# A state-space convolution beside a gated layer: other places for products, order of weights, outputs, stores and activations

## The chip, the cores and the metric

One core of a Trainium2 chip. The time is that of the whole program in device microseconds, the median of the runs shown. The engines are TensorE (PE, with its weight loads PEld), VectorE (DVE), ScalarE (ACT), GpSimd (POOL) and SyncE (SP), which here only issues transfers. ACT and POOL issue transfers too.

## What is computed

`A_u` has 2048 tokens of 448 channels. It is normalized per token, and two branches run on the result; both are added to the input.

```python
xn = _layernorm(x, axis=-1)
return x + _A_ref(xn, ...) + _B_ref(xn, ...)

# A: a long convolution per channel, its kernel a sum over 256 complex exponentials, by FFT of length 4096
K = 2.0 * jnp.einsum("dn,dnl->dl", C, P).real
Kf = jnp.fft.rfft(K, L2)
Uf = jnp.fft.rfft(u_t, L2)
y = jnp.fft.irfft(Uf * Kf[None, :, :], L2)[:, :, :L]
...
return y + u * D_skip[None, None, :]

# B: a gated layer, 448 -> 1792 -> 448
g = jnp.einsum("bsd,df->bsf", x, w_gate)
u = jnp.einsum("bsd,df->bsf", x, w_up)
h = _sigmoid(g) * u
return jnp.einsum("bsf,fd->bsd", h, w_down)
```

## The kernel before

Two Python generators, `conv` (branch A) and `glu` (branch B), write out the instructions. Each `yield` gives a weight; the loop at the end always resumes the generator whose share of its planned total is smaller. So the order in which instructions are written is a fine interleaving of the two. A planner then orders each engine's instructions: it takes what is ready by its own model of time, earlier written first (`hp(HP)` moves a piece 300 places forward). `tc.issue_after(ins)` adds an edge of order alone: what the block writes on the engine of `ins` comes behind `ins` on that engine. Each engine executes in its order.

On PE the two branches are locked into the written order by such edges: a gate's matmuls come behind `sp_mm` (the last matmul of the spectra), and those of the spectra behind `glu_mm` (the last of the gated layer).

The gated layer runs in two halves of 1024 tokens, over 14 slices `f` of 128 hidden channels in groups of 3, 3, 3, 3, 2, and for each `f` over two blocks `t` of 512 tokens. A gate (`gate`) is two *half gates* of 11 matmuls, the first for the gate and the second for the up projection, each into one of four PSUM banks `gu`. Numbers are kept in a high and a low part: a half gate first takes four matmuls with the weights' high part `wh`, then four with the low part `wl`, then three with `wh`. After both come the activation (`th` on ACT, `hf` on DVE in the PSUM bank) and its parts `hh` (ACT) and `hl` (DVE). After a group, output matmuls `po` multiply by `dh`, `dl`. In the second half the groups come in the order 6-8, 9-11, 12-13, 3-5, 0-2, and for f = 4, 5, 0, 1, 2 (`RAW`) the weights are loaded raw and split on POOL (L774, L775 for `wh`, `wl`; L802, L803 for `dh`, `dl`); for the others they are read back split.

The last part of `conv` is `spectra`, 17 steps. Step n with half h of the channels and 4 frequencies from k does, in the order written: `there` (*forward step*: 32 matmuls into PSUM `pk` from the kernel's first stage `skl`, 32 into `px` from the input's, `sx`; ACT copies the odd part to `oo`; DVE writes the sum and the difference of even and odd, `kk` (L924, L925) and `xx`); `halves` of step n-1 on DVE (`sd`); `product` of step n (DVE multiplies twice, L931 and L932; POOL subtracts, L934, and adds, L935); loads for step n+3; a pause; `back` of step n-2 (*back step*: 32 matmuls into the same PSUM, `vt` on ACT, stored to `v_d` in DRAM by SP); a pause. `turned` reads rows of `v_d` into `vp`, and `last` is the last stage of the inverse transform, added to the output tile by DVE (L998). For half 0 it comes in mid-spectra, for half 1 after all steps; the output is then stored.

Tiles of a pool with one buffer are reused: `kk`, `xx` and `yy` have one each, `sd` two.

Of the kernel before, what the change touches and what calls it, by code (L numbers as in the profile page):

```python
# [15 lines left out]
ALU = mybir.AluOpType  # L16
# [21 lines left out]
HP = 300  # L38
Y0 = (8, 1)
CP = D // 4  # L40
H = D // 2
# [86 lines left out]
def s4d_glu_kernel(ctx, tc, io):  # L128
    nc = tc.nc
# [567 lines left out]
    def gate(w, xs, to, between=None):  # L697
        wh, wl = w
        xh, xl, xr = xs
        pgu = []  # L700
        for i in range(2):
            ps = psg.tile([128, 512], F32, name="gu", bufs=4)
            mm = [(wh[:, i, k], xh[:, k]) for k in range(3)]
            mm += [(wh[:, i, 3], xr)]
            mm += [(wl[:, i, k], xh[:, k]) for k in range(3)]
            mm += [(wl[:, i, 3], xr)]
            mm += [(wh[:, i, k], xl[:, k]) for k in range(3)]
            with tc.issue_after(sp_mm[0].ins) if glu_on else nullcontext():
                for n, (a_, b_) in enumerate(mm):
                    glu_mm[:] = [nc.tensor.matmul(ps, a_, b_, start=(n == 0), stop=(n == len(mm) - 1))]  # L710
            pgu.append(ps)
            if i == 0:
                yield 2.5
                if between:
                    between()
        th = pg.tile([128, 512], F32, name="th", bufs=1)
        with hp(HP):
            marks[0] = nc.scalar.activation(th, pgu[0], AF.Tanh, scale=0.5)  # L718
        hf = pgu[1]
        with hp(HP):  # L720
            marks[1] = v.scalar_tensor_tensor(hf, th, 1.0, pgu[1], ALU.add, ALU.mult)  # L721
        hfs.append(marks[1])
        hh = pg.tile([128, 512], F32R, name="hh", bufs=2 * FCH[0])
        hl = pg.tile([128, 512], F32R, name="hl", bufs=2 * FCH[0])
        with hp(HP):
            nc.scalar.copy(hh, hf)  # L726
        with hp(HP):
            v.tensor_tensor(hl, hf, hh, ALU.subtract)  # L728
        to.append((hh, hl))

    def glu():
        stores, later, coming, coming_d = [], [], {}, {}
# [2 lines left out]
        for half in range(2):  # L735
# [4 lines left out]
            for fs_ in ORDER[half]:  # L740
# [14 lines left out]
                for n_, (f, t) in enumerate(order):  # L755
                    if t == 0:
                        wh = pg.tile([128, 2, 4, 128], F32R, name="wh", bufs=2)
                        if half == 0:
                            first = len(raws) == 2
                            raw, rd = raws.pop()  # L760
                            wl = w_low()
                            with hp(HP):
                                nc.scalar.copy(wh, raw)
                                if first:
                                    v.scalar_tensor_tensor(wl, raw, lim[:, 0, 0:1], wh, ALU.mult, ALU.subtract)
                                else:
                                    v.tensor_tensor(wl, raw, wh, ALU.subtract)
                            if not raws and f + 1 < NFT:
                                raws.append((w_load(f + 1), None))
                            if f not in RAW:  # L770
                                stores.extend(kept((wh, wl), wt_d, f))
                        elif f in RAW:
                            raw, wl = coming.pop(f), w_low()
                            nc.gpsimd.tensor_copy(wh, raw)  # L774
                            nc.gpsimd.tensor_tensor(wl, raw, wh, ALU.subtract)  # L775
                        else:
                            wl = w_low()
                            for t_, d_ in kept((wh, wl), wt_d, f):
                                nc.sync.dma_start(t_, d_)
                        if half == 1 and follow.get(f) in RAW:  # L780
                            coming[follow[f]] = w_load(follow[f], eng=nc.gpsimd)
                        ws.append((wh, wl))
                    between = (lambda s_=mid[n_]: step(*s_)) if cross and mid[n_] else None
                    yield from gate(ws[f - f0], xq[2 * half + t], hs[t], between)
                    for t_, d_ in stores:
                        nc.sync.dma_start(d_, t_)
                    stores[:] = later
                    later.clear()
                    if t == 0:
                        dh = pg.tile([128, D], F32R, name="dh", bufs=FCH[0])  # L790
                        if half == 0:
                            rd = rd or rd_load(f)
                            dl = d_low()
                            with hp(HP), tc.issue_after((act if f == 1 else marks)[0].ins):
                                nc.scalar.copy(dh, rd)
                            nc.gpsimd.tensor_tensor(dl, rd, dh, ALU.subtract)  # L796
                            if f not in RAW:
                                later.extend(kept((dh, dl), dt_d, f))
                        elif f in RAW:
                            dl = d_low()  # L800
                            rd = coming_d.pop(f)
                            nc.gpsimd.tensor_copy(dh, rd)  # L802
                            nc.gpsimd.tensor_tensor(dl, rd, dh, ALU.subtract)  # L803
                        else:
                            dl = d_low()
                            for t_, d_ in kept((dh, dl), dt_d, f):
                                nc.sync.dma_start(t_, d_)
                        if half == 1 and follow.get(f) in RAW:
                            rd = pg.tile([128, D], F32, name="rdw", bufs=1)
                            coming_d[follow[f]] = rd_load(follow[f], rd, nc.gpsimd)  # L810
                        wts.append((dh, dl))
                    yield 2.5
                    for s_ in end[n_] if cross else ():
                        step(*s_)
                    if cross:
                        yield 2
# [38 lines left out]
    def spectra(pf):  # L855
# [46 lines left out]
        def there(k, tb, sk, sx):  # L902
# [4 lines left out]
            for j, src in enumerate((sk, sx)):  # L907
# [11 lines left out]
                sp_mm[:] = [mm]  # L919
                ev, od = (half(pb[j][:np_, p, : 2 * H]) for p in range(2))  # L920
                oo = work("oo", [128, 2, H], 2)
                nc.scalar.copy(oo[:np_], od)
                t = work(("kk", "xx")[j], [128, 2, 2, H], 1)
                v.tensor_tensor(t[:np_, 0], ev, oo[:np_], ALU.add)  # L924
                read = v.tensor_tensor(t[:np_, 1], ev, oo[:np_], ALU.subtract)  # L925
                both.append(t[:np_])
            return *both, read

        def product(np_, kk, xx, eng=nc.gpsimd):
            yy = work("yy", [128, 2, 2, H], 1)[:np_]  # L930
            v.tensor_tensor(yy, kk, xx, ALU.mult)  # L931
            v.tensor_tensor(kk, kk, xx[:, :, ::-1], ALU.mult)  # L932
            with hp(HP):
                eng.tensor_tensor(yy[:, :, 0], yy[:, :, 0], yy[:, :, 1], ALU.subtract)  # L934
                eng.tensor_tensor(yy[:, :, 1], kk[:, :, 0], kk[:, :, 1], ALU.add)  # L935
            return yy

        def halves(np_, yy):
            sd = work("sd", [128, 2, 2, H], 2)
            v.tensor_tensor(sd[:np_, 0], yy[:, 0], yy[:, 1], ALU.add)  # L940
            v.tensor_tensor(sd[:np_, 1], yy[:, 0], yy[:, 1], ALU.subtract)
            return sd

        def back(h, k, sd, engs=(nc.sync, nc.sync)):
# [36 lines left out]
        def last(h, q):  # L981
# [16 lines left out]
                v.tensor_tensor(a, a, half(pb[q % 2][:, p, : 2 * H]), ALU.add)  # L998
            if h == 1 and q < 3:
                out_end(acc, 4 * q, ds, *([[nc.gpsimd]] if q == 0 else []))  # L1000
            elif h == 0 and q < 2:
                out(acc, 4 * q, h)

        ac = acl[0]
        lasts.append(last)
# [9 lines left out]
        for n, (h, k) in enumerate(steps):  # L1015
# [5 lines left out]
            if prev is not None:  # L1021
                with tc.issue_after(read.ins):
                    made = *prev[:2], halves(*prev[2:])
            prev = h, k, 64 if k == 32 else 128
            prev += (product(prev[2], kk, xx, v if end else nc.gpsimd),)
            if (h, k) == (0, ks[-NTB - 1]):
                for k_ in ks[:-NTB]:
                    tabs.pop(k_)
# [23 lines left out]
            if due and n >= due[0]:  # L1052
                sp_mm[:] = glu_mm
                for q in (0, 1, 2, 3)[2 * (n - due[0]) : 2 * (n - due[0]) + 2]:
                    sp_mm[:] = glu_mm
                    last(0, q)
                    yield WS / 2
                if n == due[0] + 1:
                    due = []
        sp_mm[:] = glu_mm  # L1060
        back(*made)
        sp_mm[:] = glu_mm
        back(*made_, (nc.sync, nc.scalar))
        for t in (*wait, made[:2], made_[:2]):
            turned(*t)

    def conv():
        with tc.tile_pool(name="psk", bufs=1, space=PSUM) as ps_, tc.tile_pool(
# [86 lines left out]
        with tc.tile_pool(name="pf", bufs=1, side="right", reuse_waits="tile") as pf:  # L1155
            yield from spectra(pf)

    lasts, glu_mm, sp_mm, glu_on, outs, x1s, hfs, xls = [], [], [], [], [0], [0], [], []
    xq, psc, raws, acl, marks, slots, pqs = list(x_first), [], [], [], [None, None], {}, []
    W1s, GGs, act = [], [], []  # L1160
    gens = [conv(), glu()]
# [42 lines left out]
```

## Time and profile before

| what | value |
|---|---|
| median of 3 runs | 746.65 us (744.72 to 747.68) |
| profiled execution | 741.93 us, span 740.1 us |
| its mean granted PE clock | 0.949 |
| PE busy over the span | 668.2 us (90%) |
| DVE, ACT, POOL busy | 587.9 (79%), 420.6 (57%), 420.8 (57%) us |
| chain that ended last | PE 40%, POOL 19%, issue 11%, DVE 11%, DMA 11% |

The profile is one execution. Its rows give start and duration in us, engine, source line (L710 is line 710 of the kernel), operation, output tile and input tiles with their shapes, how many instructions are merged, and in brackets how long the engine was idle before and what ended that. The granted clock is TensorE's, 1.00 at full speed. Forward steps of the spectra run from 542 to 699 us, the last back step to 709, the last stage of half 1 from 724 to 730.

### The profile page before, as it was taken

The page shows a single profiled execution, that of the slowest core. Times are in us where ns is not written, and L with a number is a line of the kernel's source. Part 1 is how long each engine was busy: PE and PEld are TensorE (multiplying, and loading weights), DVE is VectorE, ACT ScalarE, POOL GpSimd, SP SyncE. Part 2 cuts the span into 40 slices and gives each one's busy share as a digit, 9 for nine tenths or more (in the row PEclk, how much of TensorE's full clock was granted, in tenths as well). Part 3 has the DMA queues.
Part 4 walks back from the last instruction along what each step waited for, and adds up shares of the span by engine and source line. Part 5 has one row for each costly group of instructions (what it writes and reads, how often), then busy time and mean ns, then how long its engine had stood idle before and what let it go on. Part 6 is the DMA issues. An engine that isn't in the chain of part 4 may idle for free.

```text
span 740.1 us, 20863 instructions
## 1 busy us (share of the span) xinstructions
PE 668.2 (90%) x8581; PEld 515.1 (70%) x8581; DVE 587.9 (79%) x779; ACT 420.6 (57%) x651; POOL 420.8 (57%) x453
## 2 busy tenths in 40 slices
PE   2998999988999999788999999999988999788976
PEld 1765878866877787555878888888765667466655
DVE  5799998699999999886679898886757777756833
ACT  3655454689778789887387777777323322222310
POOL 2120116869999999974645776765537773541301
PEclk9999999995999999999999999999998989898987
DMA  9935338451313564354863323322669887874464
GB/s 199 235 114 198 116 102 263 147 188 58 126 48 97 175 191 116 114 181 148 264 188 99 93 95 95 99 81 83 157 171 266 222 244 185 262 210 130 125 169 132
DMA packets 94335, 114.47 MB, mean 155 GB/s; under 512 B 13728, under 2 KB 83936, under 8 KB 93984
## 3 DMA queue, kind: packets, MB, share of 16 engines
q1 hardware_dynamic: 72512, 92.54, 43.1%
q10 hardware_dynamic: 19248, 14.91, 7.0%
q0 software_dynamic: 2480, 5.67, 3.0%
q8 instruction: 68, 1.11, 0.6%
q14 instruction: 27, 0.22, 0.1%
HBM read 68.32 MB, written 44.76 MB: 153 GB/s over the span
## 4 chain that ended last, share of the span: by engine, by line
PE 40%; POOL 19%; issue 11%; DVE 11%; DMA 11%; SPq 5%; ACT 3%; POOLq 0%; DVEq 0%; ACTq 0%
PE gu L710 17%; PE po L831 10%; POOL me L513 7%; PE ko L619 5%; POOL mf L513 5%; PE tr L535 2%; DMA v_d<-vt 2%; POOL dl L796 2%; DVE Ft L605 2%; DVE Et L604 1%; DMA skl<-sk_d 1%; SPq L896 1%; DMA xe<-in_A_u_dram 1%; DVE Et L603 1%; POOL yy L934 1%
## 5 line engine op out<-in xcount | busy, mean ns | idle before, releaser
L513 POOL TENSOR_TENSOR me<-me,pm 128x32 f32<-128x32 f32 (+1 forms) x168 | 149.5, 890 | 67.6 <-DVE Et L604 57.8
L513 POOL TENSOR_TENSOR mf<-mf,pm 128x64 f32<-128x64 f32 (+1 forms) x112 | 118.8, 1061 | 5.3
L710 PE MATMUL gu<-xh,wh 128*128 128x512 f32 x336 | 103.2, 415 | 3.0 <-ACT th L718 1.2
L710 PE MATMUL gu<-xl,wh 128*128 128x512 f32 x336 | 97.7, 394 | 0.0
L710 PE MATMUL gu<-xh,wl 128*128 128x512 f32 x336 | 96.5, 395 | 0.0
L604 DVE TENSOR_TENSOR Et<-me,S 128x1024 f32<-128x1024 f32 x56 | 80.4, 1436 | 13.9 <-ACT me L526 9.0
L831 PE MATMUL po<-dh,hh 128*128 128x448 f32 (+1 forms) x227 | 87.4, 385 | 0.8 <-DVE acc L836 0.8
L605 DVE TENSOR_TENSOR Ft<-mf,S 128x1024 f32<-128x1024 f32 x56 | 83.8, 1496 | 5.1 <-PE ko L619 3.2
L831 PE MATMUL po<-dh,hl 128*128 128x448 f32 (+1 forms) x227 | 84.5, 374 | 2.0 <-DVE hl L728 2.0
L831 PE MATMUL po<-dl,hh 128*128 128x448 f32 (+1 forms) x227 | 84.8, 374 | 0.2 <-POOL dl L796 0.2
L603 DVE TENSOR_TENSOR Et<-me,S 128x1024 f32<-128x1024 f32 x56 | 77.5, 1385 | 4.0 <-ACT S L546 3.5
L710 PEld LDWEIGHTS gu<-xh,wh 128*128 128x128 f32 x336 | 62.6, 195 | 25.8 <-issue 6.9
L543 ACT ACTIVATE S<-tr 128x1024 f32<-128x1024 f32 x56 | 57.9, 1033 | 34.4 <-PE tr L535 18.7
L619 PEld LDWEIGHTS ko<-Et,Ft 128*32 128x32 f32 x3584 | 56.0, 114 | 28.0 <-issue 10.5
L619 PE MATMUL ko<-Et,Ft 128*32 128x64 f32 x3584 | 66.0, 227 | 9.7 <-DVE Ft L605 5.3
L710 PEld LDWEIGHTS gu<-xh,wl 128*128 128x128 f32 x336 | 63.8, 191 | 14.9 <-DVE hl L728 0.7
L710 PEld LDWEIGHTS gu<-xl,wh 128*128 128x128 f32 x336 | 63.0, 189 | 14.8 <-issue 1.4
L726 ACT CAST hh<-gu 128x512 fp32r<-128x512 f32 x56 | 33.1, 591 | 69.8 <-DVE gu L721 68.8
L836 DVE SCALAR_TENSOR_TENSOR acc<-po,acc 128x448 f32<-128x448 f32 (+1 forms) x81 | 48.7, 613 | 28.2 <-PE po L831 27.9
L934 POOL TENSOR_TENSOR yy<-yy 128x448 f32<-128x448 f32 (+1 forms) x16 | 28.5, 1778 | 67.1 <-DVE yy L931 66.9
L546 ACT ACTIVATE S<-S,hpi 128x1024 f32<-128x1024 f32 x56 | 65.6, 1171 | 0.0
L718 ACT ACTIVATE th<-gu 128x512 f32<-128x512 f32 x56 | 33.9, 606 | 43.5 <-PE gu L710 43.5
(214 smaller groups left out, 1346.7 us busy)
## 6 DMA issues: line engine op xcount, KB each, us to landing
sk_d<-sk ACTq DMA_DIRECT2D x14, 512.0 KB
sx<-x_d SPq DMA_DIRECT2D x64, 112.0 KB
skl<-sk_d SPq DMA_DIRECT2D x64, 112.0 KB
v_d<-vt SPq DMA_DIRECT2D x27, 224.0 KB
vp<-v_d SPq DMA_DIRECT2D x6, 896.0 KB
wt_d<-wh SPq DMA_DIRECT2D x9, 512.0 KB
wt_d<-wl SPq DMA_DIRECT2D x9, 512.0 KB
wl<-wt_d SPq DMA_DIRECT2D x9, 512.0 KB
```

The costliest lines, as they stand in the source:

```text
L513: ins = nc.gpsimd.tensor_tensor(m[:, :, w + a : 2 * w : n], m[:, :, a:w:n], par(base + i).unsqueeze(2).to_broadcast([128, 4 * DC, w // n]) ...
L543: nc.scalar.activation(rows(cs), pv, AF.Abs)
L546: sins[:] = [nc.scalar.activation(cs, cs, AF.Sin, scale=-TWO_PI, bias=hpi)]
L603: v.tensor_tensor(Et[:, :, :, 32:64], two(me[:, :, 32:64]), S[:, 1::-1], ALU.mult)
L604: v.tensor_tensor(Et[:, :, :, 0:32], two(me[:, :, 0:32]), S[:, 1:3, :, ::-1], ALU.mult)
L605: fts[:] = [v.tensor_tensor(Ft, two(mf), S[:, 3:5], ALU.mult)]
L619: nc.tensor.matmul(ko[32 * j : 32 * j + 32, sl], Ft[:, cc, DC * h + 4 * q + j], Et[:, cc, DC * h + 4 * q + j], start=(k == 0), stop=(k == ...
L710: glu_mm[:] = [nc.tensor.matmul(ps, a_, b_, start=(n == 0), stop=(n == len(mm) - 1))]
L718: marks[0] = nc.scalar.activation(th, pgu[0], AF.Tanh, scale=0.5)
L831: glu_mm[:] = [nc.tensor.matmul(po[:, ds], a_[:, bs], w_[:, ds], start=(n == 0), stop=(n == 3 * fc - 1))]
L836: v.scalar_tensor_tensor(acc[:, b, ds], po[:, ds], 0.5, acc[:, b, ds], ALU.mult, ALU.add)
L934: eng.tensor_tensor(yy[:, :, 0], yy[:, :, 0], yy[:, :, 1], ALU.subtract)
```

## The change

- `product` writes its second product into `xx`, no longer into `kk`, with the reversal on the other factor; `halves` writes its results into the same tile of `xx`. `xx` has three buffers and `sd` is gone.
- The activation of a gate is moved to a function `activate`. Once the spectra run, it is written one pause later than before, and `hh` comes behind ACT's last copy of forward sums (`oo`), `hl` behind DVE's last reading of them (`read`), in place of high priority.
- `wh`, `wl`, `dh`, `dl` of the raw slices come behind the last written addition (`made_by`, L935) on POOL.
- In `last` of half 0, the output of token blocks 0 to 7 is issued two pieces later, by SyncE alone; before, it went over SyncE, ScalarE and GpSimd in turn.
- At the end, one `turned` of 32 partitions is written ahead of the last two back steps and one after their stores, in place of four of 16 partitions after both.

```diff
+        if glu_on:
+            held_ops.append(lambda: activate(pgu, to))
+        else:
+            activate(pgu, to)
+
+    def activate(pgu, to):
         th = pg.tile([128, 512], F32, name="th", bufs=1)
...
-        with hp(HP):
+        with tc.issue_after(read_by[0][0].ins) if glu_on else hp(HP):
             nc.scalar.copy(hh, hf)
-        with hp(HP):
+        with tc.issue_after(read_by[0][1].ins) if glu_on else hp(HP):
             v.tensor_tensor(hl, hf, hh, ALU.subtract)
         to.append((hh, hl))
+
+    def behind():
+        return tc.issue_after(made_by[0].ins) if made_by else nullcontext()
...
                             raw, wl = coming.pop(f), w_low()
-                            nc.gpsimd.tensor_copy(wh, raw)
-                            nc.gpsimd.tensor_tensor(wl, raw, wh, ALU.subtract)
+                            with behind():
+                                nc.gpsimd.tensor_copy(wh, raw)
+                                nc.gpsimd.tensor_tensor(wl, raw, wh, ALU.subtract)
...
-                            nc.gpsimd.tensor_copy(dh, rd)
-                            nc.gpsimd.tensor_tensor(dl, rd, dh, ALU.subtract)
+                            with behind():
+                                nc.gpsimd.tensor_copy(dh, rd)
+                                nc.gpsimd.tensor_tensor(dl, rd, dh, ALU.subtract)
...
                     yield 2.5
+                    while held_ops:
+                        held_ops.pop()()
                     for s_ in end[n_] if cross else ():
...
-                nc.scalar.copy(oo[:np_], od)
-                t = work(("kk", "xx")[j], [128, 2, 2, H], 1)
+                moved = nc.scalar.copy(oo[:np_], od)
+                t = work(("kk", "xx")[j], [128, 2, 2, H], (1, 3)[j])
...
+            read_by[:] = [(moved, read)]
             return *both, read
...
             v.tensor_tensor(yy, kk, xx, ALU.mult)
-            v.tensor_tensor(kk, kk, xx[:, :, ::-1], ALU.mult)
+            v.tensor_tensor(xx, kk[:, :, ::-1], xx, ALU.mult)
             with hp(HP):
                 eng.tensor_tensor(yy[:, :, 0], yy[:, :, 0], yy[:, :, 1], ALU.subtract)
-                eng.tensor_tensor(yy[:, :, 1], kk[:, :, 0], kk[:, :, 1], ALU.add)
-            return yy
-
-        def halves(np_, yy):
-            sd = work("sd", [128, 2, 2, H], 2)
-            v.tensor_tensor(sd[:np_, 0], yy[:, 0], yy[:, 1], ALU.add)
-            v.tensor_tensor(sd[:np_, 1], yy[:, 0], yy[:, 1], ALU.subtract)
+                made_by[:] = [eng.tensor_tensor(yy[:, :, 1], xx[:, :, 0], xx[:, :, 1], ALU.add)]
+            return yy, xx
+
+        def halves(yy, sd):
+            v.tensor_tensor(sd[:, 0], yy[:, 0], yy[:, 1], ALU.add)
+            v.tensor_tensor(sd[:, 1], yy[:, 0], yy[:, 1], ALU.subtract)
             return sd
...
-            elif h == 0 and q < 2:
-                out(acc, 4 * q, h)
+            elif h == 0 and q > 1:
+                out_end(ac[:, 4 * q - 8 : 4 * q - 4], 4 * q - 8, ds, [nc.sync])
...
+        turned(*wait[0], 4)
         sp_mm[:] = glu_mm
         back(*made)
         sp_mm[:] = glu_mm
         back(*made_, (nc.sync, nc.scalar))
-        for t in (*wait, made[:2], made_[:2]):
-            turned(*t)
+        turned(*made[:2], 4)
```

More of the change, by code (lines that the diff above doesn't have):

```diff
@@ L1023, in spectra @@
                     made = *prev[:2], halves(*prev[2:])
-            prev = h, k, 64 if k == 32 else 128
-            prev += (product(prev[2], kk, xx, v if end else nc.gpsimd),)
+            prev = h, k, *product(64 if k == 32 else 128, kk, xx, v if end else nc.gpsimd)
             if (h, k) == (0, ks[-NTB - 1]):
@@ L1156, in conv @@
             yield from spectra(pf)
-    lasts, glu_mm, sp_mm, glu_on, outs, x1s, hfs, xls = [], [], [], [], [0], [0], [], []
+    held_ops, read_by, made_by, lasts, glu_mm, sp_mm, glu_on, outs, x1s, hfs, xls = [], [], [], [], [], [], [], [0], [0], [], []
     xq, psc, raws, acl, marks, slots, pqs = list(x_first), [], [], [], [None, None], {}, []
```

## The prediction, as it was put on record

> **What bounds the kernel now.** I read the stretch that the change can reach first, cut into pieces, then the waits, then each engine's rows in order of time. Nothing that the change touches runs before the spectra begin: the new places are all behind `glu_on`, `made_by` or inside `spectra`. So the question is about the last 200 us.
>
> ```profile
> 541.97:736.00 194.03, 167.77 (x2225) 119.08 (x2224) 129.64 (x193) 46.34 (x89) 81.65 (x74) 0.89 0.71 195
> 558.75:570.81 12.06, 8.78 (x107) 6.10 (x108) 9.58 (x15) 2.52 (x5) 9.13 (x10) 0.72 0.98 254
> 593.72:603.84 10.12, 8.74 (x107) 5.63 (x106) 7.43 (x12) 1.99 (x4) 5.55 (x4) 0.66 0.89 238
> 636.36:650.43 14.07, 8.83 (x108) 5.37 (x108) 8.43 (x12) 2.94 (x7) 8.87 (x8) 0.76 0.81 238
> 664.29:675.46 11.17, 8.66 (x76) 5.54 (x76) 7.06 (x10) 3.51 (x7) 2.29 (x2) 0.69 0.68 173
> 698.96:705.54 6.58, 4.82 (x46) 3.48 (x39) 6.48 (x11) 1.82 (x4) 0.02 (x1) 0.74 0.36 86
> ```
>
> Columns: length, busy PE, weight loads, DVE, ACT, POOL, then granted clock, DMA share, GB/s. PE is the bound: 167.8 of 194 us, the next engine 129.6; it idles 26 us and runs at a clock of 0.89. Much of the loss sits in five stretches, each an idle piece with several us of a clock near 0.7 after it. Two of those idle pieces:
>
> ```profile
> 595.03 0.99 PE L953 MATMUL pk<-sd,bk 32*64 32x224 f32 x16 [1.30 <-DVE kk L925]
> ```
> ```profile
> 666.72 0.99 PE L953 MATMUL pk<-sd,bk 32*64 32x224 f32 x16 [2.43 <-DVE kk L925]
> ```
>
> DMA is busy (0.71), but the waits name it little. The waits between engines that matter here (total, times, longest):
>
> ```profile
> DVE kk L924 <- POOL yy L935: 18.8, 10, 3.3
> PE pk L953 <- DVE kk L925: 10.8, 5, 5.1
> POOL dh L802 <- DMA sx<-x_d: 4.4, 1, 4.4
> ```
>
> PE waits to start a back transform until DVE has read the forward sums out of PSUM; DVE waits to write `kk` until POOL has read the old `kk` in the second addition (L935); POOL at one place stands behind a weight whose load has not landed (L802).
>
> What PE needs at full clock, from undisturbed rows (start to next start): a half gate (11 matmuls) 571.73 to 574.45 = 2.72; a forward step 574.45 to 576.12 = 1.67, half of it 0.78; a back step 650.43 to 652.41 = 1.98, or 685.30 to 686.35 = 1.05 where both banks were free and the two banks' matmuls alternate; nine output matmuls 603.84 to 605.89 = 2.05.
>
> ```profile
> 571.73 0.96 PE L710 MATMUL gu<-xh,wh 128*128 128x512 f32 x3
> 574.45 0.99 PE L918 MATMUL pk<-skl,tb 64*32 64x224 f32 x32
> 575.23 0.96 PE L918 MATMUL px<-sx,tb 64*32 64x224 f32 x32
> 576.12 0.98 PE L710 MATMUL gu<-xh,wh 128*128 128x512 f32 x3
> ```
> ```profile
> 603.84 0.47 PE L831 MATMUL po<-dh,hh 128*128 128x448 f32 x1
> 605.89 0.61 PE L953 MATMUL pk<-sd,bk 32*64 32x224 f32 x8
> ```
> ```profile
> 650.43 0.99 PE L953 MATMUL pk<-sd,bk 32*64 32x224 f32 x16
> 652.41 0.96 PE L710 MATMUL gu<-xh,wh 128*128 128x512 f32 x3
> ```
>
> **The gains, part by part.** *Products into xx, xx also as the halves' tile.* Same number of DVE and POOL instructions; memory is equal (before 1 kk, 1 xx, 1 yy, 2 sd; after 1, 3, 1, 0). `kk` is now free when DVE's own second product ends, so the ten waits of 18.8 us leave the place ahead of `kk`. The halves still need POOL's sum, but they stand four reads (2.1 us) later, longer than most of those waits. *hh and hl behind the reading of forward sums, and the whole activation one pause later*: no instruction more; it takes `hl` and its wait for ACT out of the place ahead of `kk` (1.35 us where it occurs), and `hh` out of the place ahead of `vt`. The gate's PSUM banks (4) are held at most to the next forward step, and a bank comes round only two half gates after; I cost that at nothing. *Output by SyncE*: eight stores go from three queues to SP, two pieces later; SP pays about 8 x 0.9 = 7 us of issue between 675 and 700, where its next load waits for vt anyway; ACT loses this:
>
> ```profile
> 659.49 4.71 ACTq L236 DMA_DIRECT2D out_dram<-ac  x3
> 664.30 0.60 ACT L718 ACTIVATE th<-gu 128x512 f32<-128x512 f32 x1 [7.68 <-PE gu L710]
> ```
>
> The copies of that step's forward sums stood behind these three stores and th: the 2.43 us wait at 666.72 above. With all these, each stretch shrinks toward its full-clock work:
> 558.75: 12.06 - (1.98 + 1.67 + 2.72) = 5.7.
> 593.72: 10.12 - (1.98 + 2.05 + 1.67) = 4.4.
> 636.36: 14.07 - 6.37 = 7.7; there the back step follows its forward step with no gate between, so some 1.3 us of wait (ACT copy and two reads) stays, with part of the slow clock: 5.5.
> 664.29: 11.17 - (1.98 + 2.72 + 0.78) = 5.7.
> 698.96: 6.58 - (1.98 + 1.37) = 3.2, again with no gate between: 1.5.
> A 1.4 us wait of PE at 680 for `hl` in front of the addition L998: 1.3.
> Sum 24. Six back steps may also find both banks free and take 1.05 instead of 1.98: at most 5.6, I take 4. Bounds of all this: 12 (a new wait comes at each place) to 33.
>
> *v's stores first.* SP's last rows:
>
> ```profile
> 713.61 0.52 SPq L979 DMA_DIRECT2D vp<-v_d  x1
> 714.23 0.59 SPq L973 DMA_DIRECT2D v_d<-vt  x1
> 718.87 0.52 SPq L979 DMA_DIRECT2D vp<-v_d  x1
> ```
> ```profile
> 710.11 0.67 ACTq L973 DMA_DIRECT2D v_d<-vt  x1
> ```
> ```profile
> 723.77 1.78 PE L989 MATMUL pk<-vp,wf 64*32 64x224 f32 x32 [6.84 <-issue]
> ```
>
> The last store waits on SP behind a load of `vp` that waits for the store before it to land. ACT's half of the same store went at 710.11. Without the load between, SP's half goes then too: 4.1 us earlier. The last load carries twice the rows; I take 3, bounds 0 to 5. Nothing else can start PE there, so this is on the path. Gains together: 24 + 4 + 3 = 31.
>
> **The cost: weights behind additions.** `behind()` puts five pairs wh, wl (f = 4, 5, 0, 1, 2) after the latest traced L935 on POOL. Now they are made far ahead: the pair of f = 5 at 556.8 and 558.9, its first gate at 576.12.
>
> ```profile
> 556.82 1.03 POOL L774 CAST wh<-wraw 128x1024 fp32r<-128x1024 f32 x1
> 557.82 1.14 POOL L935 TENSOR_TENSOR yy<-kk 64x448 f32<-64x448 f32 x1
> 558.92 2.35 POOL L775 TENSOR_TENSOR wl<-wraw,wh 128x1024 fp32r<-128x1024 f32 x1
> ```
>
> That wh sits ahead of an addition and delays it 1 us, which is what the edge removes. But following the generators' pauses, the pair of f is traced directly ahead of f's first half gate, and for three of the five the piece traced just before is a forward step with its product: f = 5 after the forward step at 574.45, f = 0 after the one that ends at 627.4, f = 2 after the one at 681.52. PE's rows show the same order, and PE's order is fixed by edges on both sides, so nothing can be drawn forward. The new pair must then wait for the product of that very forward step:
>
> ```profile
> 627.41 0.96 PE L710 MATMUL gu<-xh,wh 128*128 128x512 f32 x3
> ```
> ```profile
> 681.52 1.09 PE L918 MATMUL px<-sx,tb 64*32 64x224 f32 x32 [1.39 <-DVE acc L998]
> 682.54 0.98 PE L710 MATMUL gu<-xh,wh 128*128 128x512 f32 x3
> 683.59 0.85 PE L710 MATMUL gu<-xh,wl 128*128 128x512 f32 x3
> 685.30 0.42 PE L953 MATMUL pk<-sd,bk 32*64 32x224 f32 x4
> ```
> ```profile
> 683.30 0.62 DVE L924 TENSOR_TENSOR xx<-px,oo 128x448 f32<-128x448 f32 x1 [0.77 <-ACT oo L922]
> 685.56 1.09 DVE L931 TENSOR_TENSOR yy<-kk,xx 128x896 f32<-128x896 f32 x1
> ```
> ```profile
> 686.79 2.00 POOL L934 TENSOR_TENSOR yy<-yy 128x448 f32<-128x448 f32 x1 [13.02 <-DVE yy L931]
> 688.87 1.15 POOL L935 TENSOR_TENSOR yy<-kk 128x448 f32<-128x448 f32 x1
> ```
>
> This chain has no POOL wait in it, so it is the same after the change. The addition ends at 690.02; wh by 691.1 (1.03); wl by 693.5 (2.35 and 0.1 between). The half gate wants wh at 682.54; its seven matmuls from the first with wl take 683.59 to 685.30 = 1.71. It would end at 695.2, not 685.3: 9.9 us each, 29.7 for three.
>
> f = 4 is traced after the k = 32 forward step, with one half gate between:
>
> ```profile
> 548.02 1.07 PE L918 MATMUL px<-sx,t 64*32 64x224 f32 x13
> 549.02 0.97 PE L710 MATMUL gu<-xh,wh 128*128 128x512 f32 x3
> ```
>
> so 9.9 - 2.7 = 7.2. f = 1 has gate, back step, gate and a half of the last stage between (2.72 + 1.98 + 2.72 + about 1.9 = 9.3): 0.6. Sum 37.5; ends: 30 if POOL's subtraction takes the 1.1 us that it takes without DVE beside it and nothing else stands ahead, 42 if hf or hl (0.7 each) come in ahead of the products. dh and dl go behind too, but are wanted only by output matmuls a gate or more later: nothing, and it takes the 4.4 us block off POOL's additions.
>
> The four long stalls also bring the slow clock. Its price from the stretches: 10.12 - 5.70 of work - 1.30 idle = 3.1 at 593.7; 11.17 - 5.48 - 2.43 = 3.3 at 664.3. Part of it falls in the pause between wh and wl, so 2.5 each: 10, bounds 4 to 13.
>
> The Trainium skill (TensorE: Matmul & The Clock Gate, "What's actually happening") says that the clock halves after an idle window of about 3.4 us and returns after about 3.4 us of work. The trace differs on the first: a 1.3 us wait at 593.7 was followed by matmuls at half speed. By the page the short waits would cost no clock, the gains would be some 8 us smaller and the time some 8 us longer than below (770).
>
> **Sum.** 37.5 + 10 - 31 = +16.5. The profiled execution took 741.93 us (span 740.1 and 1.8 around it), 0.6% below the median 746.65 of the runs. Against the profile 758; against the median 763. As a part of the gains' bounds lies above what I took, I say 762.
>
> **Rivals.** *The weights are there in time* (faster): the additions come before PE wants the pair, and the gains stand alone: 746.65 - 31 = 716; with half of the stalls' price, 740. For it: POOL is idle 58% of the spectra (81.65 busy of 194.03), and POOL's waits ahead of additions go. Against it: 8.5 us from forward matmul to the end of the addition in the rows above, with nothing idle in the chain but 0.8 us. It decides from the point where the four stalls with their clock cost less than 31 us, 7.7 each. *Stalls and gains cancel* (no change): the subtraction at 1.1 us, no clock loss, gains at 31: 30 + 1 - 31, within 3.7 us of 746.65. *A new wait besides* (slower still): SP, with eight output stores at about 0.9, gets late with `vp`'s loads, or DMA (0.98 in the first stretch) cannot follow; the stalls give DMA time, so this is weak: 770 to 780.
>
> **How the numbers follow.** Stalls outweigh gains 0.66 (751 to 776, likeliest 762); a new wait besides 0.05; cancel 0.10; weights in time or stalls cheap 0.19. A measurement here tells about 0.5%, 3.7 us. So slower 0.71, same 0.10, faster 0.19. The range takes the upper end with some of the new wait, 777, and below reaches into the third case, 733, which leaves about 0.12 below and 0.06 above.
>
> **What would show it.** Right: POOL's L774 starts right behind an L935 in all five places; PE's largest waits are L710 on POOL's wh and wl, four of 7 to 9 us; the waits of `kk` for L935 are gone; no PE wait for `kk` at 593 and 664; ACT issues no output there; the last `vp` load starts 3 to 4 us after the last store. Wrong: gates find wl made before the forward step ahead of them, or PE does other matmuls in the stalls.

## The result, and the profile after

The changed kernel takes 765.87 us (762.85 to 767.58, 4 runs) beside 747.16 us (744.72 to 749.35, 4 runs) of the kernel before: ratio 1.0247, 95% interval [1.02, 1.0293]. It is slower by 18.7 us; 762 was predicted. The profiled execution took 765.31 us, its span 763.5 us against 740.1 before. In the changed kernel `wh` and `wl` are written at L784 and L785, the addition is L949, the reading of the forward sums L937 and L938, the back step L966, the forward step L931, `vt` L972, v's stores L986, its loads L992.

The waits of TensorE from 541 us on, first before, then after (engine and line that waits, what it waits for: total, times, longest):

```profile
PE pk L953 <- DVE kk L925: 10.8, 5, 5.1
PE pk L989 <- issue: 6.8, 1, 6.8
PE pk L918 <- ACT vt L959: 1.7, 1, 1.7
```
```profile
PE gu L710 <- POOL wh L784: 34.0, 5, 9.2
PE pk L1002 <- DMA vp<-v_d: 4.0, 1, 4.0
PE gu L710 <- POOL wl L785: 3.9, 5, 1.3
PE pk L931 <- ACT vt L972: 2.5, 3, 1.4
PE pk L966 <- DVE kk L938: 1.3, 1, 1.3
```

The change did what it says: of the 10.8 us ahead of back steps 1.3 are left, and the 6.8 us ahead of the last stage are 4.0. In their place stand 37.9 us ahead of half gates, for `wh` and `wl`. All five places, PE's rows in order of time (f = 4, 5, 0, 1, 2):

```profile
560.01 1.65 PE L710 MATMUL gu<-xh,wh 128*128 128x512 f32 x3 [5.91 <-POOL wh L784]
590.73 1.65 PE L710 MATMUL gu<-xh,wh 128*128 128x512 f32 x3 [9.21 <-POOL wh L784]
593.55 1.65 PE L710 MATMUL gu<-xh,wl 128*128 128x512 f32 x3 [0.75 <-POOL wl L785]
649.88 1.65 PE L710 MATMUL gu<-xh,wh 128*128 128x512 f32 x3 [8.74 <-POOL wh L784]
677.02 0.97 PE L710 MATMUL gu<-xh,wh 128*128 128x512 f32 x3 [1.31 <-POOL wh L784]
679.47 0.98 PE L710 MATMUL gu<-xh,wl 128*128 128x512 f32 x3 [1.26 <-POOL wl L785]
705.44 1.65 PE L710 MATMUL gu<-xh,wh 128*128 128x512 f32 x3 [8.87 <-POOL wh L784]
```

POOL's rows at the second place show why: the pair stands right behind the addition, and it is the addition of the forward step that PE has just done.

```profile
586.52 1.97 POOL L948 TENSOR_TENSOR yy<-yy 128x448 f32<-128x448 f32 x1 [3.60 <-DVE yy L945]
588.57 1.13 POOL L949 TENSOR_TENSOR yy<-xx 128x448 f32<-128x448 f32 x1
589.64 1.04 POOL L784 CAST wh<-wraw 128x1024 fp32r<-128x1024 f32 x1
590.62 0.56 POOL L813 CAST dh<-rdw 128x448 fp32r<-128x448 f32 x1
591.14 2.36 POOL L785 TENSOR_TENSOR wl<-wraw,wh 128x1024 fp32r<-128x1024 f32 x1
```

Stretches around the last long stall, of the changed kernel (length, busy PE, weight loads, DVE, ACT, POOL, granted clock, DMA share, GB/s):

```profile
710.00:712.00 2.00, 2.00 (x16) 1.05 (x23) 0.00 (x0) 0.29 (x1) 0.00 (x0) 0.50 0.00 0
712.00:714.00 2.00, 2.00 (x38) 1.42 (x23) 0.00 (x0) 1.28 (x3) 0.00 (x0) 0.98 0.00 0
```

PE started again at 705.44, and the clock stayed at 0.50 until about 712. From 700 to 714 DMA stands nearly still too (a share of 0.02 at most). At the second and the third stall, between 584 and 590.7 and between 644 and 650, it does not: its share was 0.49 to 1.11, so transfers go on while PE waits.

### The profile page after: what moved, and what is told of

Same layout as the page of the kernel before. It is cut to its first block, busy times and chain, and to the rows that moved or that the text cites. A ratio compares the mean times of both kernels' runs of the same rounds, so it can differ in the third digit from the quotient of the medians.

```text
span 763.5 us, 20858 instructions
## 1 busy us (share of the span) xinstructions
PE 669.3 (88%) x8581; PEld 514.6 (67%) x8581; DVE 582.9 (76%) x779; ACT 420.9 (55%) x651; POOL 418.2 (55%) x450
## 3 DMA queue, kind: packets, MB, share of 16 engines
q8 instruction: 68, 1.11, 0.6%
## 4 chain that ended last, share of the span: by engine, by line
PE 47%; POOL 16%; issue 10%; DVE 10%; DMA 8%; ACT 4%; SPq 3%; POOLq 0%; DVEq 0%; ACTq 0%
PE gu L710 19%; PE po L844 11%; POOL me L513 6%; PE ko L619 5%; POOL mf L513 4%; PE tr L535 2%; POOL dl L806 2%; PE pk L931 2%; PE pk L966 2%; POOL wl L785 2%; DMA rd<-in_B_w_down_dram 1%; DMA xe<-in_A_u_dram 1%; DVE Et L604 1%; PE px L931 1%; DVE Ft L605 1%
## 5 line engine op out<-in xcount | busy, mean ns | idle before, releaser
L513 POOL TENSOR_TENSOR me<-me,pm 128x32 f32<-128x32 f32 (+1 forms) x168 | 151.7, 903 | 74.5 <-DVE Et L604 64.7
L710 PE MATMUL gu<-xh,wh 128*128 128x512 f32 x336 | 106.2, 425 | 36.5 <-POOL wh L784 34.0
L513 POOL TENSOR_TENSOR mf<-mf,pm 128x64 f32<-128x64 f32 (+1 forms) x112 | 114.7, 1024 | 5.3
L710 PEld LDWEIGHTS gu<-xh,wh 128*128 128x128 f32 x336 | 64.2, 201 | 60.8 <-POOL wh L784 36.2
L710 PE MATMUL gu<-xh,wl 128*128 128x512 f32 x336 | 99.8, 406 | 3.9 <-POOL wl L785 3.9
L710 PE MATMUL gu<-xl,wh 128*128 128x512 f32 x336 | 100.4, 404 | 0.0
L727 DVE SCALAR_TENSOR_TENSOR gu<-th,gu 128x512 f32<-128x512 f32 x56 | 38.5, 688 | 64.7 <-PE gu L710 60.1
L605 DVE TENSOR_TENSOR Ft<-mf,S 128x1024 f32<-128x1024 f32 x56 | 80.0, 1429 | 4.9 <-PE ko L619 4.4
L948 POOL TENSOR_TENSOR yy<-yy 128x448 f32<-128x448 f32 (+1 forms) x16 | 30.5, 1906 | 93.8 <-DVE yy L945 93.8
L710 PEld LDWEIGHTS gu<-xl,wh 128*128 128x128 f32 x336 | 65.2, 195 | 15.6 <-issue 1.4
```

The costliest lines, as they stand in the source:

```text
L513: ins = nc.gpsimd.tensor_tensor(m[:, :, w + a : 2 * w : n], m[:, :, a:w:n], par(base + i).unsqueeze(2).to_broadcast([128, 4 * DC, w // n]) ...
L605: fts[:] = [v.tensor_tensor(Ft, two(mf), S[:, 3:5], ALU.mult)]
```

## The experiments

My theory is the prediction's: the edge costs about 47 us, the other parts bring about 31. The rival: both are much smaller, and only their difference is right. The parts of the change can be built apart.

**The edge taken out, and the edge alone.** In the first run `behind()` orders nothing:

```diff
     def behind():
-        return tc.issue_after(made_by[0].ins) if made_by else nullcontext()
+        return nullcontext()
```

> The changed kernel without the edge: wh, wl, dh, dl may stand anywhere on POOL again. Theory (the pairs come late, everything else gains): PE's waits for wh and wl go, 765.9 - 49 (five half gates lengthened by 9.0, 12.7, 12.2, 3.0, 12.3) = 717; weights in front of additions may give some back: 715 to 728. Rival (the other parts cost time as well and the edge is only a part of the loss): 740 or more.

In the second, the kernel before has `behind()` around `wh`, `wl`, `dh`, `dl`, its L935 fills `made_by`, and nothing else is changed.

> The kernel before with the edge alone. Theory: the same five stalls, 37.5 + 10 for the clock = 47 on top of 747, less some 5 where POOL's additions no longer stand behind dh: 785 to 800. Rival (the stalls come only together with the held activations or the products in xx): under 770.

Measured, with 741.35 us for the kernel before: without the edge 730.09 us, ratio 0.9815 [0.9756, 0.9875]; the edge alone 775.94 us, ratio 1.0445 [1.0385, 1.0504]. The edge makes the kernel slower by 4.4% on the kernel before, where PE then waits 38.8 us for `wh` and `wl`, and by as much on the other parts (1.0247 / 0.9815 = 1.044). That is some 33 us by these ratios, not 47; and the other parts bring 1.85%, some 14 us, not 31. Both runs miss what the theory gave them, in the direction of the rival: the signs are right, the sizes are not. TensorE's waits with the edge taken out, from 541 us on:

```profile
PE pk L931 <- ACT vt L972: 9.1, 4, 4.2
PE pk L1002 <- DMA out_dram<-acc: 2.9, 1, 2.9
PE pk L931 <- DMA skl<-sk_d: 2.9, 1, 2.9
PE pk L931 <- DMA vp<-v_d: 1.7, 1, 1.7
PE pk L966 <- DVE kk L938: 1.3, 1, 1.3
```

The stalls for weights are gone, and a wait has come that hardly stood in the other two lists: 9.1 us of forward steps for `vt`. Nearly all of it, 8.1 us, is two waits, each behind a copy of ScalarE into `vt` that had waited for a store:

```profile
623.85 1.85 PE L931 MATMUL pk<-skl,tb 64*32 64x224 f32 x32 [4.15 <-ACT vt L972]
642.58 1.85 PE L931 MATMUL pk<-skl,tb 64*32 64x224 f32 x32 [3.92 <-ACT vt L972]
```
```profile
623.26 0.53 ACT L972 COPY vt<-pk 128x448 f32<-128x448 f32 x1 [8.20 <-DMA v_d<-vt]
641.99 0.53 ACT L972 COPY vt<-pk 128x448 f32<-128x448 f32 x1 [5.96 <-DMA v_d<-vt]
```

Two more copies waited for stores, 3.05 us at 602.55 and 4.98 at 611.52, and PE did not wait for those. `vt` has two buffers. A copy waits until the store of two steps earlier has landed, PE's next forward step waits for the copy, since it takes the same PSUM. By the rows the store is late because SyncE issues it late. SP's rows in the same run:

```profile
603.72 1.24 SPq L986 DMA_DIRECT2D v_d<-vt  x2
611.49 0.51 SPq L992 DMA_DIRECT2D vp<-v_d  x1
612.10 2.14 SPq L909 DMA_DIRECT2D skl<-sk_d  x4
614.34 2.59 SPq L902 DMA_DIRECT2D sx<-x_d  x4
617.17 1.79 SPq L982 DMA_DIRECT2D v_d<-vt  x2
619.06 2.53 SPq L984 DMA_DIRECT2D v_d<-vt  x4
```

What was copied at 602.98 begins to be stored at 617.17. SP stood until 611.49 in the load of `vp` that waits for the store of 603.72 to land, then issued the inputs of later steps; the copy at 623.26 then waited for the last of these stores. The landing is a part of it too: the store of 603.72 took 7.8 us, with a DMA share of 0.99 from 603 to 608. So full DMA engines stay a rival to the order in SP's queue.

**Where the edge may stand.** Two other places of it in the changed kernel: on `dh`, `dl` alone, and for all four behind the addition one step earlier.

```diff
-                            with behind():
-                                nc.gpsimd.tensor_copy(wh, raw)
-                                nc.gpsimd.tensor_tensor(wl, raw, wh, ALU.subtract)
+                            nc.gpsimd.tensor_copy(wh, raw)
+                            nc.gpsimd.tensor_tensor(wl, raw, wh, ALU.subtract)
```

> The changed kernel with the edge on dh and dl alone; wh and wl free. Theory: as e1, and POOL's additions never stand behind a dh that waits for its load (4.4 us in the kernel before): 712 to 724, equal to e1 or up to 5 faster. Rival (dh and dl behind the addition make output matmuls wait): slower than e1 by 3 or more.

```diff
-        return tc.issue_after(made_by[0].ins) if made_by else nullcontext()
+        return tc.issue_after(made_by[-2].ins) if len(made_by) > 1 else nullcontext()
...
-                made_by[:] = [eng.tensor_tensor(yy[:, :, 1], xx[:, :, 0], xx[:, :, 1], ALU.add)]
+                made_by.append(eng.tensor_tensor(yy[:, :, 1], xx[:, :, 0], xx[:, :, 1], ALU.add))
```

> The changed kernel with the edge to the addition of the step before the last written one. Theory (the latency from the forward step to the addition makes the loss): the pair is ready 1 to 3 us after PE wants it for f = 4 and 0, some 5 for f = 5, not late for f = 1 and 2: 717 + 10 + clock 4 = 725 to 737. Rival (any edge costs, by POOL's fixed order): as the changed kernel, above 755.

Measured, `dh` and `dl` alone: 731.43 us, 0.9845 [0.979, 0.9899]; one step earlier: 733.19 us, 0.9855 [0.9773, 0.9936]. So `dh` and `dl` may stand behind the addition at no price that can be told, as predicted (the range of 712 to 724 was missed, since it rested on gains of 31), and one addition earlier nearly all of the price is gone: the cost lies in waiting for the product of the very last forward step, not in POOL's order as such. PE's waits with the edge one step back:

```profile
PE gu L710 <- POOL wl L785: 4.8, 3, 1.6
PE gu L710 <- POOL wh L784: 3.3, 2, 2.2
PE pk L931 <- ACT vt L972: 0.5, 1, 0.5
```

8.1 us for weights are left, and the 9.1 us for `vt` are nearly gone; the time can't be told from that of the run without the edge. It looks as if one wait stood for the other. That 733 lies in the 725 to 737 of the theory is luck: it added a price of 14 to a kernel of 717, where some 3 on 730 were measured.

**The other four parts, each alone on the kernel before.** The products and the halves in `xx`; the activations one pause later and behind `oo` and `read`; half 0's output by SyncE; v's stores ahead of its last load. Each is its own lines of the diff shown above, with nothing of `behind()`.

> The kernel before with the products' places alone (second product and halves in xx, xx three buffers). Theory: the ten waits of kk for POOL (18.8 us) go; PE's gaps at 558, 593 and part of 636 shrink; hl and ACT's output stay in the way: 747 - 10 (6 to 16) = 731 to 741. Rival (the wait only moves to the halves): 747 within 3.

> The kernel before with the held activations alone (hh and hl behind the reading of forward sums). Theory: kk no longer stands behind hl at 680 and 699, vt not behind hh at 562; kk still waits for POOL: 747 - 5 (1 to 9) = 738 to 746. Rival (the PSUM banks are held longer and gates wait): 750 or more.

> The kernel before with the output of half 0 by SyncE alone, two pieces later. Theory: ACT's 4.7 us of issue at 659 go, PE's wait of 2.4 us at 664 and its slow clock of 3.3 too: 747 - 5 = 740 to 744. Rival (SP's 7 us of issue delay loads and v's rows): 747 within 3 or slower.

> The kernel before with v's stores first alone. Theory: the last store goes 4.1 us earlier, the last load carries twice the rows: 747 - 3 = 742 to 746. Rival (the larger load takes back what the order gains): 747 within 1.5.

Measured beside 742.26 us: 743.42 us, 1.0026 [0.9993, 1.006]; 741.63 us, 0.9996 [0.9963, 1.0029]; 738.5 us, 0.9959 [0.9926, 0.9991]; 740.21 us, 0.9975 [0.9946, 1.0005]. The products, of which I had expected the most, bring nothing that can be told by themselves, and neither do the activations; the output brings 0.4%, v's stores about 2 us, at the edge of what can be told. (The ranges above start from 747, but the kernel before took 742.26 us here; the ratios are what counts.) Added up the four give 0.4%, together they gave 1.85%. The products alone, DVE's, PE's and ScalarE's waits:

```profile
DVE kk L924 <- ACT oo L922: 25.5, 9, 9.0
PE pk L952 <- DVE kk L925: 8.8, 3, 5.4
PE pk L918 <- ACT vt L958: 10.5, 5, 3.6
ACT vt L958 <- DMA v_d<-vt: 18.3, 3, 7.7
```

Before, `kk` waited 18.8 us for POOL's L935 and 9.7 for `oo`. Now it waits 25.5 for `oo` alone. PE's wait for the reading of the forward sums falls only from 10.8 to 8.8, and the wait for `vt` is there with 10.5 (1.7 before). ScalarE's copies into `vt` wait 18.3 us for stores, which they did not do at all before. So the wait did move, as the rival said, but not to the halves.

**v's loads one step later.** If the load of `vp` holds up SP, it should help to write it a step later; in the changed kernel, where the stalls give the stores time, it should do nothing.

```diff
-            while len(wait) > 2 and not (due and wait[0][0] == 1):
+            while len(wait) > 3 and not (due and wait[0][0] == 1):
```

> The change without its order edge (as in the run that took 0.9815 of before), and v's loads back from DRAM issued one step later, so that SyncE's queue no longer stands in a load that waits for the store issued just before it. Theory (the gains that stayed out are held up by the order in SyncE's queue: there, loads waited 23.6 us for stores, ScalarE's copies into vt 22.2 us for the stores of two steps earlier, and TensorE 22.1 us for these copies): about half of TensorE's 22 us goes, so 10 us off, 0.963 to 0.972 of before (about 715 to 721). Rival (the stores are slow because the DMA engines carry too much, not because of the order): within 3 us of the run without the edge, 0.978 to 0.986.

> The changed kernel with its edge, and v's loads one step later. Theory (the edge's stalls cost 49 us gross and only some 35 net, because they give the stores the time that is otherwise waited for): no such wait is there to be removed, so no more than 3 us change from the changed kernel, 1.02 to 1.03 of before. Rival (the load order costs with the edge as well): 8 us or more off, 1.015 or less.

> The edge set one addition earlier (the run that took 0.9855 of before), and v's loads one step later. Its profile without the later loads shows ScalarE's copies into vt waiting 2.9 us for stores and TensorE 1.3 us for these copies. Theory: little is to be had, 0 to 4 us off, 0.980 to 0.987 of before. Rival: as much as without the edge, 10 us off, 0.972 or less.

Measured, each against the kernel before at 743.24 us: 732.55 us, 0.9858 [0.9819, 0.9898]; 766.63 us, 1.0316 [1.0272, 1.036]; 735.24 us, 0.9902 [0.9873, 0.9932]. No gain anywhere; the second and the third lie just beyond their theory's range, on the slow side. The theory of the first also had its 22.1 us wrong: that is 9.1 us of waits of the matmuls and 13.0 of the weight loads for the same copies, which run side by side, so at most some 9 us were to be had. But the runs don't decide whether the order in SP's queue is the cause: in the order that the planner made of it, SP's queue is unchanged up to the output stores near 664 us, and only two loads after them move. The waits stand where they stood; the run without the edge and with this line has:

```profile
ACT vt L972 <- DMA v_d<-vt: 23.9, 5, 7.4
PE pk L931 <- ACT vt L972: 10.5, 5, 3.7
```

**v's stores by ScalarE.** This takes the stores out of SP's queue altogether, in the kernel without the edge:

```diff
-                back(*ready)
+                back(*ready, (nc.scalar, nc.scalar))
```

> The change without its order edge (the run that took 0.9815 of before), and v's stores in the loop issued by ScalarE right behind the copies into vt, not by SyncE behind loads. In that run the copy of 587.5 us had its store issued at 597.9, that of 603.0 at 617.2: SyncE stood in the load of v for the store before, then in the loads of the next steps. Theory (the gains that stayed out are held up by the order in SyncE's queue): ScalarE's waits in vt for stores go from 22.2 us to under 6, TensorE's waits for vt from 22.1 to under 10; against it stand some 1.3 us of ScalarE for each step's two issues, ahead of the next copies into oo; 5 to 12 us off, 0.966 to 0.976 of before (717 to 724). Rival (the stores land late because the DMA engines are full, wherever they are issued): the waits in vt stay at 15 us or more and the time within 3 us of that run or above it, 0.978 or more.

Measured: 746.52 us beside 741.06, ratio 1.0069 [1.0029, 1.0109]; slower than without this edit by some 2.5%. The wait that it was to remove has gone from the list: no copy into `vt` waits for a store. But PE waits as long for `vt` as it did, 9.3 us, and others came. ScalarE's rows at the first such store:

```profile
560.57 0.54 ACT L972 COPY vt<-px 128x448 f32<-128x448 f32 x1
566.48 1.62 ACTq L986 DMA_DIRECT2D v_d<-vt  x2
568.14 0.53 ACT L935 COPY oo<-pk 128x448 f32<-128x448 f32 x1 [7.03 <-DMA sx<-x_d]
```

The store could go at 561.1 and goes at 566.48, behind a load of `sx`. The built program of this run, the list of instructions that each engine got, shows why. All transfers of SP's and ScalarE's queues take eight counters in turn, and an issue first waits until the transfer that had its counter before, eight issues ago, has landed. The first store has the counters of two loads of `sx`, those that SP issued from 561.08 on (shortened; the numbers count each engine's instructions):

```
SP 423 sx<-x_d [waits counter 1, PE]
SP 424 sx<-x_d [waits counter 2]
...
ACT 615 v_d<-vt [waits counter 1, ACT]
ACT 616 v_d<-vt [waits counter 2]
```

So a store on ScalarE brings the waits for loads into ScalarE's queue. `kk` then waited 43.9 us for `oo`, against 23.9 in the run without this edit, and PE for `kk` 11.1 us again:

```profile
DVE kk L937 <- ACT oo L935: 43.9, 17, 7.2
PE pk L966 <- DVE kk L938: 11.1, 4, 4.7
PE px L931 <- ACT vt L972: 9.3, 2, 5.5
```

That the 9 us for `vt` can be had by a better order of transfers is therefore not shown, nor that SP's order is what makes the stores late. A third buffer of `vt` needs 3.5 KB for each partition, more than this pool has left; no run has one.

**The account.** The stretch from the first forward step to the end, by profile: its length is PE's busy time, its waits and some 5 us between single matmuls. The first forward step begins at 541.97 us in the kernel before, at 544.35 in the changed kernel and at 542.92 without the edge; where these 1 to 2 us ahead of it come from is open, and they are left out here. PE's busy time in the stretch (first number of busy time), in this order:

```profile
541.97:765.00 223.03, 167.77 (x2225) 119.08 (x2224) 130.03 (x193) 46.34 (x89) 81.65 (x74) 0.90 0.63 171
```
```profile
544.35:765.00 220.65, 162.91 (x2225) 115.68 (x2224) 127.70 (x193) 46.49 (x89) 93.15 (x85) 0.87 0.63 177
```
```profile
542.92:765.00 222.08, 158.12 (x2225) 115.85 (x2224) 130.15 (x193) 46.38 (x89) 79.19 (x71) 0.93 0.60 172
```

| | before | without the edge | changed |
|---|---|---|---|
| first forward step to end of the span | 198.1 | 184.4 | 219.2 |
| PE busy | 167.8 | 158.1 | 162.9 |
| PE's waits, all lines of the list | 25.4 | 21.5 | 50.8 |
| the rest | 5.0 | 4.8 | 5.4 |

The four other parts: 13.8 us off, of which 9.7 are shorter matmul time (a clock of 0.93 in place of 0.90, back steps whose two banks alternate) and 3.9 fewer waits. The edge: 34.8 us on, of which 29.3 are waits and 4.8 matmul time at a lower clock. Each kernel's profile is one execution; the runs' ratios gave 14 and 33.

## Why the prediction was right, and where two terms were not

The time (762 against 765.87) and the direction were right, and the mechanism is shown by its removal: the edge alone costs 4.4%. Of the signs named, the pairs stand right behind the addition at all five places, no `kk` waits for the addition any more, and the four long waits were 5.9, 9.2, 8.7 and 8.9 us, where four of 7 to 9 were named. But that the time came so close is luck: the cost was 35 where 47.5 stood, the gains 14 where 31 stood, and the two errors cancel in part (+16.5 predicted, +21 by the account). The rest is the comparison: the four runs of the kernel before beside the result took 747.16, while its later medians were 741.06 to 743.24.

*The stalls, step by step.* The chain that set them was right: predicted 8.5 us from the start of the last half forward step on PE to the end of the addition, measured 9.1 at f = 5 (580.56 to 589.70; `hl` at 584.70 came in ahead of the product). From the half gates' ends, their lengthening with the slow clock was 8.8, 12.7, 12.2, 3.0 and 12.3 us for f = 4, 5, 0, 1, 2: 49.0 together, against 37.5 + 10 = 47.5 predicted; f = 1 was to take 0.6. `dh` came in between `wh` and `wl` at three of them (0.56 us), which I had not seen.

*What failed: "37.5 + 10" as a cost in the sum.* Of these 49 us only some 35 appear in the time. I had put the stalls on top of a kernel without waits. Without the edge PE waits 21.5 us elsewhere, with it 50.8 - 37.9 = 12.9: 8.6 us of other waits, above all for `vt`, are absent. The stores land while PE stands: ScalarE's copies into `vt` wait 22.2 us for stores without the edge, and not at all in the changed kernel. The edge alone, on the kernel before, likewise takes PE's waits for `kk` ahead of back steps from 10.8 to 4.2 us. The slow clock, too, is partly there without the edge: PE's forward steps behind the waits of 4.15 and 3.92 us for `vt` took 1.85 per half in place of 0.97. The steps "the stalls give DMA time" and "a new wait besides" were both in the prediction, but the first one stood there only as a reason against the second, without a price.

*What failed: "Sum 24" of the stretches, mis-sized.* It took each stretch down to its work at full clock, as if nothing were late next, with a lower bound of 12 for "a new wait comes at each place". All the gains together measured 13.8 us where 31 were taken. The shorter wait ahead of the last stage is 3.9 of them, the back steps are about 4.7 (an estimate: seven ran bank after bank before and two without the edge, at 1.98 - 1.05 each), so some 5 are left for the 24. PE's waits ahead of everything but the last stage did not shrink at all: 25.4 - 6.8 = 18.6 before, 21.5 - 2.9 = 18.6 without the edge. One by one: PE's waits for `kk` ahead of back and forward steps fell from 12.0 to 2.5 us; but those for `vt` came up from 2.4 to 9.8, for `skl` and `vp` from 1.3 to 4.6, and 1.3 for `hh` is new. Some 2.5 us of other waits went. Ahead of the last stage 6.8 became 2.9. What was late next after `kk` was the landing of v's stores; that SP's queue holds them back is read from its rows, and no run confirms it. The prediction gave moving the output to SP a cost of nothing beyond 7 us of issue (5.2 measured), and asked of SP only whether its loads come late, not its stores. The wait for `vt` does not hang on that part, though: the products alone bring it too (10.5 us). The four parts also aren't a sum of parts: alone they give 0.4%, together 1.85%.

*v's stores first:* 3 us predicted; from the last copy of a back step to the last stage it was 13.7 us before and is 10.8 after, 2.9 less. The row of the stage in the changed kernel, whose wait is now the load itself:

```profile
746.83 1.78 PE L1002 MATMUL pk<-vp,wf 64*32 64x224 f32 x32 [3.99 <-DMA vp<-v_d]
```

*The clock.* The price of a long stall was about right: 0.50 for 6.6 us after the last one, and at all five places the lengthening is 49.0 - 37.9 = 11 us beyond the waits, where 10 were taken. The price of a short one is no constant. In the changed kernel two waits of 1.31 and 1.26 us follow one another and cost no clock, while the 1.30 us wait of before at 595.03 was followed by 0.59. Stretches of the changed kernel, then of the kernel before:

```profile
676.00:678.00 2.00, 0.98 (x4) 0.67 (x4) 2.00 (x4) 0.00 (x0) 1.92 (x2) 1.00 0.87 227
678.00:680.00 2.00, 0.74 (x3) 0.48 (x3) 0.03 (x1) 0.00 (x0) 1.71 (x2) 1.00 0.64 169
680.00:682.00 2.00, 2.00 (x38) 1.34 (x44) 0.00 (x0) 0.52 (x1) 2.00 (x4) 1.00 0.97 235
```
```profile
596.00:598.00 2.00, 1.92 (x20) 1.23 (x18) 1.97 (x3) 0.00 (x0) 0.00 (x0) 0.59 1.09 248
```

The wait at 595.03 is not alone: before, the granted clock fell to 0.51 and 0.54 after the waits of 2.43 us at 666.72 and 1.68 at 700.70, and in the changed kernel to 0.50 after that of 1.27 at 726.64. All four stand ahead of a back step that runs bank after bank, but so does the 1.27 us wait at 663.35 of the changed kernel, and there the clock stayed at 1.00; what else slows the clock is open.

The Trainium skill (TensorE: Matmul & The Clock Gate, "What's actually happening") speaks of an idle window of about 3.4 us. Here the waits of 1.3 us at 677 and 679 and those of 3.9 us and more agree with it, the four named above don't. By that rule the gains would have been taken some 8 us lower, nearer to what was measured, but not for the reason measured, since the clock did fall; its time of 770 is as far from 765.87 as 762.

## What to carry to other kernels

An order edge that puts work behind "the latest written" instruction costs the whole latency of that instruction's chain where the work is wanted right behind it: here 9 us, and 9 to 13 us of lengthening at four of five places. Put one step back, it left 8.1 us of waits and no price that could be told. A stall's price in the sum is its length less the waits that it takes away elsewhere, so a cost and a gain that share a resource can't be sized apart: here 49 us of lengthening were some 35 us of time. Before a removed wait is counted as a gain, look for what is late next on each queue behind it, stores as well as loads.

The fastest version measured is the change without its edge: 0.9815 [0.9756, 0.9875] of the kernel before, 730.09 us; with the edge on `dh` and `dl` alone it can't be told from that.

## What had not been expected of the hardware

Matmuls do not always slow down after a short wait: the same 1.3 us was followed by a granted clock of 1.00 at 677 and 679 of the changed kernel and by 0.59 from 596 to 598 of the kernel before. A transfer's issue can hold the engine that issues it for longer than the transfer's own cost: ScalarE stood from 561.1 to 566.48 before a store whose issue takes 0.8 us, because the built program lets it wait for an earlier load. And two banks in turn make 32 small matmuls of a back step take 1.05 us where 1.98 were needed one bank after the other; by the estimate above about 4.7 of the 9.7 us of matmul time that the change saves without the edge come from that.
